# A linear-attention and SwiGLU block on one core: VectorE's side work by weight, earlier layer-norm of tiles 8 to 15, SyncE in written order, another place for wo

## The chip, the cores and the metric

One core of one Trainium2 chip. The metric is the device time of one execution in microseconds (us). TensorE is called PE, its weight loads PEld, VectorE DVE, ScalarE ACT, GpSimd POOL, SyncE SP; a `q` behind a name (SPq) is that engine's DMA issue. The kernel before takes 760.22 us, the median of three runs (759.44, 760.22 and 761.99).

## The reference

```python
xn = layernorm(x)                                  # x: 2048 tokens x 1024
q, k, v = split(xn @ wqkv)                         # 32 heads of 32
phi = lambda t: where(t > 0, t + 1, exp(t)) + 1e-6
kv  = einsum("bhsd,bhse->bhde", phi(k), v)         # sums over all tokens
z   = einsum("bhsd->bhd", phi(k))
o   = (phi(q) @ kv) / (phi(q) @ z + 1e-6)
s   = o @ wo
g   = silu((silu(xn @ w_gate) * (xn @ w_up)) @ w_down)   # hidden 3584
out = x + s * g
```

## The kernel before, in words

The 2048 tokens are 16 tiles of 128; four tiles are a block of 512 (block 2 is tiles 8 to 11, block 3 is tiles 12 to 15), two blocks are a pass of 1024. Three stages follow one another: the front (layer-norm, K, V, their sums, most of Q; about 0 to 163 us), the attention output (163 to 246 us), and the feed-forward part (from 246 us). The change lies in the front and at its seam with the attention output.

**Layer-norm.** `emit_stats` (line 331) takes a tile's statistics in two halves on DVE, `emit_aggr` (344) joins them, `emit_rstd` (358) gives 1/sqrt by three Newton steps on POOL or on DVE for a whole group of tiles (blocks 2 and 3 are one group each), and `emit_norm` (379) writes the normalised tile into `ws_all` as scratch. Tiles 0 to 7 are then turned by PE (`emit_T`, transposes at 405, copied out by DVE at 419 and ACT at 420). Blocks 2 and 3 are turned by DMA instead: `emit_xT_block` (422) stores the block to `xn_dram` (423) and loads it back transposed into `xnT` (424), both on SP.

**K and V, plain.** `emit_B(i, c)` (461) is eight matmuls of 512 columns (440) of tile i with column chunk c of the weights: c 0 and 1 are K, 2 and 3 are V. ACT makes exp and relu of K (186, 187), DVE joins them to phi (190, 191), ACT copies V (458). `emit_C(i)` (465) adds the tile to the sums `kvz` in PSUM. The loop over `rest` does so for tiles 4 to 7, 8 and 12.

**Q, K, V by seven products.** From tile 12's turn on, `QGroup` (211), and `KVGroup` (508) for tiles t of blocks 2 and 3 together, compute a 2x2 block product by seven products (Strassen-Winograd form) with sums of operands made beforehand on DVE: of the tokens (`xsum_ops`, 134, five operations of 128x2048), of wq (`wsum_ops`, 148, four smaller ones for each group), and of the K and V weights (`kv_sum_ops`, 487, five of 128x2048 each, two of them in place). `KVGroup(0, t)` is K of tiles 8+t and 12+t, `KVGroup(1, t)` is V of them; `VPlain` (709) is V of tiles 9 and 13 by plain matmuls. Each group has parts a, b, c and `post`; a group's part c is emitted behind part a of the next.

**What sets the order.** Under `tc.manual_schedule(engines=FRONT_ORDER)` (608) the instructions of PE, DVE, ACT and POOL stand in the order in which the code emits them; SP's order in the front is left to the scheduler, which puts both stores to `xn_dram` ahead of both transposes. DVE's side work (statistics, norms and sums of blocks 2 and 3) lies in a queue `later`; `fill(n)` (602) takes n operations from it, and the calls of `fill` between matmul groups, with the tables `fills` (678) and `seq` (727), spread them. In `seq` the groups come as Q1, K1, VPlain, Q2, K2, V2, Q3, K3, Q(1,0), V3, Q(1,1); a pair of tiles is added to `kvz` when its V is done.

**The seam.** The pools of the front close (`p1`) and those of the attention output open in their place (`p2`, 751): `otp`, `work`, `small`, then `wop` with wo. SP loads wo in two halves (846). `emit_ND` (774) divides and writes `o_sb` (795); `emit_OT` (804) stores it to `o_dram` (ACT, 808) and loads it back transposed (SP, 809); `emit_S` (814) multiplies by wo (822).

Of the kernel before, what the change touches and what calls it, by code (L numbers as in the profile page):

```python
# [12 lines left out]
BF16 = mybir.dt.bfloat16  # L13
# [8 lines left out]
def kernel(  # L22
# [11 lines left out]
    nc = tc.nc  # L34
    P = 128
    x2 = A_x.flatten_outer_dims()
    out2 = out.flatten_outer_dims()
    S, D = x2.shape
# [4 lines left out]
    DC = D // P  # L43
# [3 lines left out]
    NB = S // TB  # L47
# [61 lines left out]
    def xn_tok_ap(i):  # L109
        return xnT[i * P // SP_TOK][:, :, i * P % SP_TOK: i * P % SP_TOK + P]  # L110
# [153 lines left out]
    with ExitStack() as p1:  # L264
# [1 line left out]
        work = p1.enter_context(tc.tile_pool(name="p1work", bufs=4))  # L266
        small = p1.enter_context(tc.tile_pool(name="p1small", bufs=4))

        wkv_sb = wpool.tile([P, DC, 2 * D], BF16, name="wkv_sb")
        NV = 4  # L270
        v_bufs = [wpool.tile([P, G, NDW], BF16, name=f"v_sb{k}") for k in range(NV)]
        for k in range(NV):
# [11 lines left out]
        def load_x(i):  # L284
# [5 lines left out]
            eng = nc.scalar if i == 1 else nc.sync  # L290
            x_loads[i] = eng.dma_start(out=x_ap(i), in_=x2[i * P:(i + 1) * P, :])

        def load_wkv(c, halves=1):
            hs = DC // halves
            return [nc.sync.dma_start(out=wkv_sb[:, h * hs:(h + 1) * hs, c * CW:(c + 1) * CW],
                                      in_=wqkv_v[:, h * hs:(h + 1) * hs, D + c * CW: D + (c + 1) * CW])
                    for h in range(halves)]

# [27 lines left out]
        def emit_stats(i, parts=None):  # L326
            if i not in part_stats:
                part_stats[i] = small.tile([P, NSC, nc.vector.BN_STATS_DIM], FP32, name="stats", tag="stats")
            xr = x_ap(i).rearrange("p (c f) -> p c f", f=SCH)
            for c in (range(NSC) if parts is None else parts):  # L330
                nc.vector.bn_stats(out=part_stats[i][:, c, :], in_=xr[:, c, :])  # L331
            if parts is None:
                emit_aggr(i)

        def emit_aggr(i):
            gid = grp_of[i]
            tiles = GROUPS[gid]
            if gid not in grp_state:
                mv = small.tile([P, TPB, AGG], FP32, name="mv", tag="mv")
                rstd = small.tile([P, TPB], FP32, name="rstd", tag="rstd")  # L340
                grp_state[gid] = (mv, rstd, tiles)
            mv, rstd, _ = grp_state[gid]
            k = tiles.index(i)
            nc.vector.bn_aggr(out=mv[:, k, :], in_=part_stats.pop(i)[:])
            ln_state[i] = (mv, rstd, k)
# [44 lines left out]
        def xn_blk_slot(b):  # L390
            o = xn_base + b % 2 * TPB * D
            return ws_flat[:, o:o + TPB * D].rearrange("p (t d) -> p t d", t=TPB).bitcast(FP16)
# [44 lines left out]
        def emit_B_mm(i, c):  # L437
            kv_ps = psB.tile([P, CW], FP32, name="kv_ps", tag="B")
            for dc in range(DC):
                mm = nc.tensor.matmul(kv_ps[:], lhsT=xn_tok_ap(i)[:, dc, :], rhs=wkv_sb[:, dc, c * CW:(c + 1) * CW],  # L440
                                      start=(dc == 0), stop=(dc == DC - 1))
                if dc == 0 and c == 0:
                    marks[("B", i)] = mm
            kv_tiles[(i, c)] = kv_ps
# [40 lines left out]


        def kv_sum_ops(which, places):
            w = wkv_sb[:, :, which * D:(which + 1) * D]
            w11, w12, w21, w22 = w[:, 0:HD, 0:CW], w[:, 0:HD, CW:D], w[:, HD:DC, 0:CW], w[:, HD:DC, CW:D]
            s1, s5, s2 = places  # L490
            kv_rhs[which] = {"M4": lambda k: w22[:, k, :], "M3": lambda k: w11[:, k, :], "M1": lambda k: s1[:, k, :],
                             "M5": lambda k: s5[:, k, :], "M2": lambda k: s2[:, k, :],
                             "N7": lambda k: w21[:, k, :], "N6": lambda k: w12[:, k, :]}
            tt = nc.vector.tensor_tensor
            return [lambda: tt(out=s1, in0=w11, in1=w22, op=ALU.add), lambda: tt(out=s5, in0=w11, in1=w21, op=ALU.add),
                    lambda: tt(out=s2, in0=w12, in1=w22, op=ALU.add),
                    lambda: tt(out=w21, in0=w22, in1=w21, op=ALU.subtract),
                    lambda: tt(out=w12, in0=w11, in1=w12, op=ALU.subtract)]
# [9 lines left out]
        class KVGroup:  # L508
# [54 lines left out]
            def post(self):  # L563
                if self.which == 0:
                    for j in range(2):
                        emit_phi(self.pk[j][:], self.e[j][:])
                        pk_tiles[self.tiles[j]] = self.pk[j]
                else:
                    ready_C.extend(self.tiles)

        ready_C = deque()


        later = deque()

        def stats_ops(b):
            ops = []
            for i in range(b * TPB, (b + 1) * TPB):
                ops.append(lambda i=i: emit_stats(i, parts=(0,)))
                ops.append(lambda i=i: (emit_stats(i, parts=(1,)), emit_aggr(i)))  # L580
            return ops

        def norm_ops(b):
            return [lambda t=t: emit_norm(b * TPB + t, xn_blk_slot(b)[:, t, :]) for t in range(TPB)] + [lambda: emit_xT_block(b)]

        def ws_ops(m):
            return wsum_ops(wq_sb[:, :, m * FW:(m + 1) * FW], ws_all[:, m // 2, m % 2])

        later.extend(stats_ops(NB - 2) + [lambda: emit_rstd((NB - 2) * TPB)] + stats_ops(NB - 1))
        later.extend([lambda: emit_rstd((NB - 1) * TPB, nc.vector), None, None])  # L590
        for ops in (norm_ops(NB - 2), norm_ops(NB - 1), xsum_ops(0), ws_ops(0)):
            later.extend(ops)

        def more_ops():

            alloc_pqT()
            k_ops = kv_sum_ops(0, (pq_place(NPASS - 1, NM_Q - 2), pq_place(NPASS - 1, NM_Q - 1), x_quarter(0, 0, 1)))
            v_ops = kv_sum_ops(1, (x_quarter(0, 1, 0), x_quarter(1, 0, 1), x_quarter(1, 1, 0)))
            for ops in (ws_ops(1), xsum_ops(NPASS - 1), k_ops, v_ops[:1], ws_ops(2), v_ops[1:], ws_ops(3)):
                later.extend(ops)  # L600

        def fill(n):
            for _ in range(n):
                op = later.popleft() if later else None
                if op:
                    op()

        with tc.manual_schedule(engines=FRONT_ORDER):

            warm_up(14)  # L610
            emit_stats(0, parts=(0,))
# [26 lines left out]
            emit_B_mm(2, 0)  # L638
            emit_B_out(1, 2)
            emit_B_mm(2, 1)  # L640
            emit_T(3)
            emit_stats(TPB)
            emit_stats(TPB + 1)
            emit_rstd(TPB)
            emit_B_out(2, 0)
# [17 lines left out]
            emit_C(2)  # L663
            emit_B_out(3, 0)
            emit_B_mm(3, 1)
            emit_T(TPB)
            emit_B_out(3, 1)
            emit_N(TPB + 2)
# [6 lines left out]
            fill(2)  # L675

            rest = list(range(TPB, 2 * TPB)) + [b * TPB for b in range(2, NB)]
            fills = {2 * TPB: (2, 2, 1, 1), rest[-1]: (2, 2, 1, 1)}
            before = TPB - 1
            for i in rest:  # L680
                nf = fills.get(i, (3, 2, 2, 2))
                if i == 2 * TPB:
                    more_ops()
                grp = QGroup(0, 0) if i == rest[-1] else None
                emit_B(i, 0)
                fill(nf[0])
                emit_C(before)
                before = i
                if grp:
                    grp.part_a()  # L690
                emit_B(i, 1)
                fill(nf[1])
                if grp:
                    grp.part_b()
                if i == TPB:
                    emit_T(TPB + 2)
                emit_B(i, 2)
                fill(nf[2])
                if i == TPB:
                    emit_T(TPB + 3)  # L700
                if grp:
                    grp.part_c()
                emit_B(i, 3)
                if grp:
                    grp.post()
                fill(nf[3])

            K, V = (lambda t: KVGroup(0, t)), (lambda t: KVGroup(1, t))
            class VPlain:
# [7 lines left out]
                        emit_B(i, c)  # L717

                def part_c(self):
                    ready_C.extend(tiles1)  # L720

                def post(self):
                    pass

            tiles1 = [(NB - 2 + j) * TPB + 1 for j in range(2)]
            Q = QGroup
            seq = [(lambda: Q(0, 1), 1, 1), (lambda: K(1), 0, 1), (VPlain, 2, 2), (lambda: Q(0, 2), 1, 1),
                   (lambda: K(2), 1, 1), (lambda: V(2), 2, 2), (lambda: Q(0, 3), 0, 0), (lambda: K(3), 0, 0),
                   (lambda: Q(NPASS - 1, 0), 0, 0), (lambda: V(3), 0, 0), (lambda: Q(NPASS - 1, 1), 0, 0)]
            prev = None  # L730
            for make, fa, fb in seq:
# [17 lines left out]
        gate(wq_loads, marks[("B", 3)], sync=True)  # L749

    with ExitStack() as p2:
        otp = p2.enter_context(tc.tile_pool(name="p2oT", bufs=1))
        work = p2.enter_context(tc.tile_pool(name="p2work", bufs=2))
        small = p2.enter_context(tc.tile_pool(name="p2small", bufs=2))
        wop = p2.enter_context(tc.tile_pool(name="wop", bufs=1))
        oT_ab = otp.tile([P, 2, G, TB], BF16, name="oT")
        oT_cd = wq_sb[:].rearrange("p c n -> p (c n)").rearrange("p (b g t) -> p b g t", b=2, t=TB)
        s_tiles = {}
# [496 lines left out]
```

## Time and profile before

| | |
|---|---|
| median of three runs | 760.22 us |
| the profiled execution | 760.91 us |
| its span, first to last instruction | 759.1 us |
| PE busy | 743.6 us (98%) |
| DVE busy | 507.5 us (67%) |
| ACT busy | 275.9 us (36%) |
| POOL busy | 50.1 us (7%) |
| mean granted clock of PE | 0.996 |

The profiled execution is 0.69 us above the median, and 1.8 us of it lie outside the span. The share of busy time is taken over the whole program; single gaps of PE must be looked for in the view of waits (who waited for whom, in all, how often, longest) and then in the timeline (start, length, engine, line, operation, output<-input, count, and in brackets the idle time before it with what ended it). The view by stretches gives for each stretch the length, the busy time of PE, PEld, DVE, ACT and POOL with counts, then the granted clock, the DMA share and GB/s.

### The profile page before, as it was taken

What the parts mean: (1) busy time and instruction counts of PE and PEld (TensorE: products, weight loads), DVE (VectorE), ACT (ScalarE), POOL (GpSimd) and SP (SyncE); (2) the same over time, 40 slices, a digit from 0 to 9 for tenths busy, and PEclk for the clock granted to TensorE, in tenths of its full rate; (3) what the DMA queues carried; (4) which work ended last, traced back from release to release, by engine and by line L of the source; (5) the groups of instructions that cost most, each with busy time, mean ns of one, the idle gap of its engine ahead of it and who ended that gap; (6) DMA issues with size and microseconds to landing.
All of it is one profiled execution on the core that took longest, in us unless ns stands there. A gap on an engine that the chain in (4) does not pass through costs nothing.

```text
span 759.1 us, 9917 instructions
## 1 busy us (share of the span) xinstructions
PE 743.6 (98%) x3704; PEld 350.8 (46%) x3744; DVE 507.5 (67%) x939; ACT 275.9 (36%) x483; POOL 50.1 (7%) x101
## 2 busy tenths in 40 slices
PE   9998999998999999999999999999999999999997
PEld 4543444454554444444444444444444444444454
DVE  6697697686772578777687777776755754455453
ACT  4443475655423443343434334343433111111111
POOL 3310000000000000000000000000000221212220
PEclk9999999999999999999999999999999999999999
DMA  9608000035589635473354634553969854444300
GB/s 316 221 17 215 8 1 0 1 97 154 152 226 271 184 97 167 149 215 105 115 174 145 194 103 141 160 160 111 298 209 345 319 180 180 180 180 150 113 28 29
DMA packets 127664, 115.99 MB, mean 153 GB/s; under 512 B 29440, under 2 KB 108416, under 8 KB 126336
## 3 DMA queue, kind: packets, MB, share of 16 engines
q1 hardware_dynamic: 122720, 106.58, 44.8%
q10 hardware_dynamic: 4896, 8.78, 3.3%
q8 instruction: 29, 0.48, 0.2%
q14 instruction: 19, 0.16, 0.1%
HBM read 70.52 MB, written 38.54 MB: 144 GB/s over the span
## 4 chain that ended last, share of the span: by engine, by line
PE 91%; DVE 4%; DMA 3%; ACT 1%; issue 1%; DVEq 0%; ACTq 0%
PE X L131 29%; PE Y L131 28%; PE Z L131 10%; PE s_ps L822 7%; PE kv_ps L440 6%; PE qY L131 2%; PE qX L131 2%; PE kY L131 1%; PE kX L131 1%; DMA xnT<-xn_dram 1%; PE nd_ps L785 1%; PE kvz L469 1%; DVE stats L331 1%; DMA o_dram<-o_sb 1%; PE qZ L131 1%
## 5 line engine op out<-in xcount | busy, mean ns | idle before, releaser
L131 PEld LDWEIGHTS <-ws_all 128*128 128x128 bf16 x1420 | 137.6, 98 | 161.8 <-issue 0.2
L918 DVE TENSOR_TENSOR q<-n,Y 128x512 f32<-128x512 f32 x63 | 43.3, 688 | 107.7 <-PE Y L131 104.0
L131 PEld LDWEIGHTS <-xs 128*128 128x128 bf16 (+1 forms) x716 | 67.6, 98 | 75.3 <-issue 1.2
L440 PE MATMUL kv_ps<-wkv_sb,xnT 128*128 128x512 bf16 x342 | 79.8, 383 | 3.8 <-DMA xnT<-xn_dram 2.8
L1188 POOL TENSOR_TENSOR o_out<-y,xres 128x512 bf16<-128x512 f32 x29 | 35.1, 1212 | 669.1 <-DVE y L1187 669.1
L131 PE MATMUL Y<-xs,ws_all 128*128 128x512 f16 (+3 forms) x308 | 70.3, 360 | 0.0
L131 PE MATMUL X<-xnT,ws_all 128*128 128x512 f16 (+1 forms) x278 | 70.1, 379 | 0.2
L131 PE MATMUL Z<-xs,ws_all 128*128 128x512 f16 x224 | 57.5, 379 | 0.0
L131 PE MATMUL Y<-xnT,ws_all 128*128 128x512 f16 x224 | 57.5, 379 | 0.0
L131 PE MATMUL X<-xs,ws_all 128*128 128x512 f16 x224 | 57.5, 379 | 0.0
L1042 ACT ACTIVATE g<-cg 128x512 bf16<-128x512 f32 x56 | 35.3, 630 | 53.7 <-DVE cg L933 53.7
L924 DVE TENSOR_TENSOR u<-Z,q 128x512 f32<-128x512 f32 x63 | 43.3, 687 | 16.0 <-PE Z L131 15.9
L440 PEld LDWEIGHTS <-xnT 128*128 128x128 f16 x352 | 33.9, 99 | 42.7 <-DMA xnT<-xn_dram 3.3
L1042 ACT ACTIVATE g<-X 128x512 bf16<-128x512 f32 x28 | 16.7, 597 | 99.7 <-PE X L131 99.7
L914 ACT COPY n<-X 128x512 f32<-128x512 f32 x63 | 36.9, 585 | 28.7 <-PE X L131 28.7
L1067 DVE TENSOR_TENSOR ho<-g,up 128x1024 bf16<-128x1024 bf16 x56 | 38.2, 686 | 0.5
L1187 DVE TENSOR_TENSOR y<-y,s_in 128x512 f32<-128x512 f32 x31 | 22.2, 717 | 20.7 <-ACT y L1181 15.8
L131 PEld LDWEIGHTS <-wg_sb 128*128 128x128 bf16 x224 | 21.9, 98 | 26.4
L131 PEld LDWEIGHTS <-wu_sb 128*128 128x128 bf16 x224 | 21.9, 98 | 26.4
L826 ACT CAST s_sb<-s_ps 128x512 bf16<-128x512 f32 x32 | 18.5, 585 | 40.8 <-PE s_ps L822 36.1
L822 PE MATMUL s_ps<-wo_sb,oT 128*128 128x512 bf16 x123 | 29.0, 379 | 3.2 <-DMA oT<-o_dram 3.0
L1181 ACT ACTIVATE y<-X 128x512 f32<-128x512 f32 x8 | 4.8, 597 | 69.7 <-PE X L131 61.2
(173 smaller groups left out, 1101.9 us busy)
## 6 DMA issues: line engine op xcount, KB each, us to landing
h_dram<-ho SPq DMA_DIRECT2D x56, 256.0 KB, 2.5
wg_sb<-in_B_w_gate_dram SPq DMA_DIRECT2D x14, 512.0 KB, 3.9
wu_sb<-in_B_w_up_dram SPq DMA_DIRECT2D x14, 512.0 KB, 4.2
wdr<-in_B_w_down_dram SPq DMA_DIRECT2D x14, 512.0 KB, 4.0
ws_all<-h_dram SPq DMA_DIRECT2D x4, 1792.0 KB, 9.0
wds_dram<-wdsA SPq DMA_DIRECT2D x14, 384.0 KB, 2.6
hp_a<-h_dram SPq DMA_DIRECT2D x3, 1792.0 KB, 7.3
o_dram<-o_sb ACTq DMA_DIRECT2D x16, 256.0 KB, 2.9
```

The lines of the kernel that those rows point to most:

```text
L131: marks["mm"] = nc.tensor.matmul(acc[:, 0:c1 - c0], lhsT=lhs(k), rhs=rhs(k)[:, c0:c1], start=(first and k == 0), stop=(k == n - 1), skip_g ...
L331: nc.vector.bn_stats(out=part_stats[i][:, c, :], in_=xr[:, c, :])
L440: mm = nc.tensor.matmul(kv_ps[:], lhsT=xn_tok_ap(i)[:, dc, :], rhs=wkv_sb[:, dc, c * CW:(c + 1) * CW], start=(dc == 0), stop=(dc == DC - 1))
L822: mm = nc.tensor.matmul(s_ps[:], lhsT=oT[:, c, ttok], rhs=wo_sb[:, c, cc * CW:(cc + 1) * CW], start=(c == 0), stop=(c == G - 1))
L826: nc.scalar.copy(out=s_sb[:, cc * CW:(cc + 1) * CW], in_=s_ps[:])
L914: nc.scalar.copy(out=n[:], in_=self.X[:])
L918: nc.vector.tensor_tensor(out=self.q[:], in0=n[:], in1=self.Y[:], op=ALU.add)
L924: nc.vector.tensor_tensor(out=self.u[:], in0=Z[:], in1=self.q[:], op=ALU.add)
L1042: nc.scalar.activation(out=self.g[:, i, j * TB:(j + 1) * TB], in_=src, func=ACT.Silu)
L1067: nc.vector.tensor_tensor(out=self.ho[:, i], in0=self.g[:, i], in1=self.up[:, i], op=ALU.mult)
L1187: nc.vector.tensor_tensor(out=t[:], in0=t[:], in1=self.s_in[:, i, cs], op=ALU.mult)
L1188: (nc.vector if last and (i, j) != (0, 0) else nc.gpsimd).tensor_tensor(out=self.o_out[:, i, cs], in0=t[:], in1=self.xres[:, i, cs], op=AL ...
```

## The change

- `later` now holds pairs of a weight and an operation. `fill(n)` adds n to a credit and takes operations, each paid with its weight, while the credit is above zero. Statistics and norms weigh 1, DVE's Newton steps 4, wq's sums 0.75, the 128x2048 sums 2, the DMA turn of a block 0.
- Queue order: statistics of block 2, its 1/sqrt (POOL), statistics of block 3, norms of block 2 with its turn, 1/sqrt of block 3 (DVE), norms of block 3 with its turn, then all sums.
- `emit_stats(TPB)` (tile 4) moves ahead of the copy of tile 3's transpose, and a new `fill(4)` stands ahead of the copy of tile 4's transpose.
- `seq` becomes Q1, VPlain, K1, Q2, V2, K2, Q3, K3, Q(1,0), V3, Q(1,1), with other fills; a pair of tiles is now added to `kvz` when both its K and its V are done (`have`).
- SP, too, stands in written order in the front: store of block 2, its transpose, store of block 3, its transpose.
- `wkv_sb` is split into `wk_sb` and `wv_sb`, and `wop` is the first pool of `p2`, so that `wo_sb` gets the bytes of `wk_sb`.

The instructions of PE, ACT and POOL are the same in number and kind; on DVE they are too. Their order changes.

```diff
-        wkv_sb = wpool.tile([P, DC, 2 * D], BF16, name="wkv_sb")
+        wkv_sb = [wpool.tile([P, DC, D], BF16, name=n) for n in ("wk_sb", "wv_sb")]
...
-                else:
-                    ready_C.extend(self.tiles)
+                have(self.tiles)
 
         ready_C = deque()
+        half = set()
+
+        def have(tiles):
+
+            if tiles[0] in half:
+                ready_C.extend(tiles)
+            half.add(tiles[0])
...
-        later.extend(stats_ops(NB - 2) + [lambda: emit_rstd((NB - 2) * TPB)] + stats_ops(NB - 1))
-        later.extend([lambda: emit_rstd((NB - 1) * TPB, nc.vector), None, None])
-        for ops in (norm_ops(NB - 2), norm_ops(NB - 1), xsum_ops(0), ws_ops(0)):
-            later.extend(ops)
...
-            for ops in (ws_ops(1), xsum_ops(NPASS - 1), k_ops, v_ops[:1], ws_ops(2), v_ops[1:], ws_ops(3)):
-                later.extend(ops)
-
-        def fill(n):
-            for _ in range(n):
-                op = later.popleft() if later else None
-                if op:
-                    op()
-
-        with tc.manual_schedule(engines=FRONT_ORDER):
+        def put(weight, ops):
+            later.extend((weight, op) for op in ops)
+
+        def fill(n):
+            credit[0] += n
+            while later and credit[0] > 0:
+                weight, op = later.popleft()
+                credit[0] -= weight
+                op()
...
+            put(2, xsum_ops(0))
+            put_ws(0)
+            put_ws(1)
+            put(2, xsum_ops(NPASS - 1))
+            put(2, k_ops)
+            put_ws(2)
+            put(2, v_ops[:1])
+            put_ws(3)
+            put(2, v_ops[1:])
+
+        put_stats(NB - 2)
+        put(1, [lambda: emit_rstd((NB - 2) * TPB)])
+        put_stats(NB - 1)
+        put_norms(NB - 2)
+        put(4, [lambda: emit_rstd((NB - 1) * TPB, nc.vector)])
+        put_norms(NB - 1)
+        put(0, [put_sums])
+
+        with tc.manual_schedule(engines=FRONT_ORDER | {ET.SP}):
...
             emit_B_mm(2, 1)
+            emit_stats(TPB)
             emit_T(3)
-            emit_stats(TPB)
...
             emit_B_mm(3, 1)
+            fill(4)
             emit_T(TPB)
...
-            fills = {2 * TPB: (2, 2, 1, 1), rest[-1]: (2, 2, 1, 1)}
+            fills = {rest[-1]: (2, 3, 2, 2)}
...
-                if i == 2 * TPB:
-                    more_ops()
...
                 def part_c(self):
-                    ready_C.extend(tiles1)
+                    have(tiles1)
...
-            seq = [(lambda: Q(0, 1), 1, 1), (lambda: K(1), 0, 1), (VPlain, 2, 2), (lambda: Q(0, 2), 1, 1),
-                   (lambda: K(2), 1, 1), (lambda: V(2), 2, 2), (lambda: Q(0, 3), 0, 0), (lambda: K(3), 0, 0),
+            seq = [(lambda: Q(0, 1), 1, 1), (VPlain, 4, 6), (lambda: K(1), 1, 1), (lambda: Q(0, 2), 1, 1),
+                   (lambda: V(2), 3, 3), (lambda: K(2), 1, 1), (lambda: Q(0, 3), 1, 0), (lambda: K(3), 0, 0),
...
     with ExitStack() as p2:
+        wop = p2.enter_context(tc.tile_pool(name="wop", bufs=1))
         otp = p2.enter_context(tc.tile_pool(name="p2oT", bufs=1))
         work = p2.enter_context(tc.tile_pool(name="p2work", bufs=2))
         small = p2.enter_context(tc.tile_pool(name="p2small", bufs=2))
-        wop = p2.enter_context(tc.tile_pool(name="wop", bufs=1))
```

More of the change, by code (lines that the diff above doesn't have):

```diff
@@ L291, in load_x, with wkv_ap @@
             x_loads[i] = eng.dma_start(out=x_ap(i), in_=x2[i * P:(i + 1) * P, :])
+        def wkv_ap(c):
+            return wkv_sb[c // NCC][:, :, c % NCC * CW:(c % NCC + 1) * CW]
         def load_wkv(c, halves=1):
             hs = DC // halves
-            return [nc.sync.dma_start(out=wkv_sb[:, h * hs:(h + 1) * hs, c * CW:(c + 1) * CW],
+            return [nc.sync.dma_start(out=wkv_ap(c)[:, h * hs:(h + 1) * hs, :],
                                       in_=wqkv_v[:, h * hs:(h + 1) * hs, D + c * CW: D + (c + 1) * CW])
@@ L439, in emit_B_mm @@
             for dc in range(DC):
-                mm = nc.tensor.matmul(kv_ps[:], lhsT=xn_tok_ap(i)[:, dc, :], rhs=wkv_sb[:, dc, c * CW:(c + 1) * CW],
+                mm = nc.tensor.matmul(kv_ps[:], lhsT=xn_tok_ap(i)[:, dc, :], rhs=wkv_ap(c)[:, dc, :],
                                       start=(dc == 0), stop=(dc == DC - 1))
@@ L487, in kv_sum_ops @@
         def kv_sum_ops(which, places):
-            w = wkv_sb[:, :, which * D:(which + 1) * D]
+            w = wkv_sb[which]
             w11, w12, w21, w22 = w[:, 0:HD, 0:CW], w[:, 0:HD, CW:D], w[:, HD:DC, 0:CW], w[:, HD:DC, CW:D]
@@ L567, in post, with put_stats, put_norms, put_ws @@
                         pk_tiles[self.tiles[j]] = self.pk[j]
-                else:
-                    ready_C.extend(self.tiles)
+                have(self.tiles)
         ready_C = deque()
-        later = deque()
-        def stats_ops(b):
-            ops = []
-            for i in range(b * TPB, (b + 1) * TPB):
[L579 to L587, printed above, removed]
-        later.extend(stats_ops(NB - 2) + [lambda: emit_rstd((NB - 2) * TPB)] + stats_ops(NB - 1))
-        later.extend([lambda: emit_rstd((NB - 1) * TPB, nc.vector), None, None])
-        for ops in (norm_ops(NB - 2), norm_ops(NB - 1), xsum_ops(0), ws_ops(0)):
-            later.extend(ops)
-        def more_ops():
+        half = set()
[3 more added lines that the diff above has]
+            half.add(tiles[0])
+        later = deque()
+        credit = [0]
+        def put(weight, ops):
[6 more added lines that the diff above has]
+                op()
+        def put_stats(b):
+            for i in range(b * TPB, (b + 1) * TPB):
+                put(1, [lambda i=i: emit_stats(i, parts=(0,)), lambda i=i: (emit_stats(i, parts=(1,)), emit_aggr(i))])
+        def put_norms(b):
+            put(1, [lambda t=t: emit_norm(b * TPB + t, xn_blk_slot(b)[:, t, :]) for t in range(TPB)])
+            put(0, [lambda: emit_xT_block(b)])
+        def put_ws(m):
+            put(0.75, wsum_ops(wq_sb[:, :, m * FW:(m + 1) * FW], ws_all[:, m // 2, m % 2]))
+        def put_sums():
             alloc_pqT()
```

## The prediction, made before the changed kernel ran

> **What bounds the kernel now.** The page comes first: PE is busy for 98% of the span, and the change neither adds nor removes an instruction on any engine. It can gain only where PE stands still or runs at a lower clock, so the next view is that of PE's waits.
>
> ```profile
> PE 743.6 (98%) x3704; PEld 350.8 (46%) x3744; DVE 507.5 (67%) x939; ACT 275.9 (36%) x483; POOL 50.1 (7%) x101
> ...
> PE s_ps L822 <- DMA oT<-o_dram: 3.0, 1, 3.0
> PE kv_ps L440 <- DMA xnT<-xn_dram: 2.8, 1, 2.8
> ```
>
> Two waits matter, each happens once, and both are for a DMA transpose. The stretches around the second line (length, busy PE, PEld, DVE, ACT, POOL, granted clock, DMA share, GB/s) show its price:
>
> ```profile
> 65.00:70.67 5.67, 5.67 (x33) 2.58 (x30) 5.57 (x8) 2.76 (x5) 0.00 (x0) 1.00 1.10 271
> 70.67:73.50 2.83, 0.01 (x2) 0.01 (x1) 2.25 (x6) 0.58 (x1) 0.00 (x0) 1.00 1.07 208
> 73.50:77.42 3.92, 3.70 (x16) 2.02 (x18) 0.00 (x0) 0.68 (x2) 0.00 (x0) 0.56 0.95 215
> ```
>
> PE is idle for 2.83 us before tile 8, and then works at a mean clock of 0.56: in quarter-microsecond stretches the clock is 0.50 from 74.0 to 77.4. Half a clock for 3.42 us loses 1.7 us. **Gap 1 costs 4.5 us.** The timeline says why the transpose is late:
>
> ```profile
> 58.14 1.91 DVE L379 TENSOR_SCALAR ws_all<-xp,mv,rstd 128x1024 f16<-128x1024 bf16 x4
> 60.07 3.91 SPq L423 DMA_DIRECT2D xn_dram<-ws_all  x2
> 61.66 1.91 DVE L379 TENSOR_SCALAR ws_all<-xp,mv,rstd 128x1024 f16<-128x1024 bf16 x4
> 64.45 10.66 SPq L424 DMA_TRANSPOSE xnT<-xn_dram  x2
> ```
>
> The norms of block 2 end at 60.05, its store lands 4.4 us later, and its transpose, beside the store of block 3 (issued 63.59), takes 9.0 us more. The chain, for both gaps:
>
> ```profile
> 60.07 4.36 DMA xn_dram<-ws_all
> 64.45 9.01 DMA xnT<-xn_dram
> ...
> 168.37 6.17 DMA o_dram<-o_sb
> 174.56 3.54 DMA oT<-o_dram
> ```
>
> Gap 2 (175.16 to 178.14, 2.98 us, clock 1.00 throughout) waits for the first `o_sb`, whose store takes 6.2 us, against 2.9 in the median of its kind, because wo's 2 MB (issued from 163.62) use the DMA engines.
>
> **Part 1: statistics and norms sooner.** I walked DVE's new order with old durations. It puts work into two idle stretches:
>
> ```profile
> 21.20:23.57 2.37, 2.32 (x17) 1.32 (x17) 0.00 (x1) 0.00 (x0) 0.00 (x0) 1.00 1.03 379
> 32.90:35.75 2.85, 2.85 (x26) 1.78 (x25) 0.01 (x1) 1.08 (x2) 1.99 (x11) 1.00 1.02 343
> ```
>
> A tile's statistics take 1.39 us (starts at 39.72, 41.16, 42.55). Tile 4's fit the first stretch. Tiles 8 and 9 (2.8 us) fit the second; since tile 4's moved up, they may begin 1.2 us earlier, so the copies of both transposes stay on time. The x loads are issued by 21.0 and their traffic is over by about 26. If that cover were short, PE would notice only beyond several microseconds, as tile 4's matmuls begin at 41.68. From 39.72 DVE goes: tiles 10, 11 to 42.6; three 1/sqrt operations of 0.2 to 43.2; tile 12 to 44.6; phi 1.2 to 45.8; tile 13 to 47.1; a copy; tile 14 to 48.85; a copy; tile 15 to 50.6. POOL's twelve Newton operations (0.28 apart) run from 43.2 to 46.6, beside this. Three norms of 0.48 end at 52.0, a phi that waits for ACT (53.15, as now) ends at 54.4, the fourth norm at 54.9, against 60.05. So the store lands at 54.9 + 4.4 = 59.3 and the transpose 6.5 to 9.0 us later (the two rows of L424), at 65.8 to 68.3. PE needs it at 70.67. Gap 1 goes with its clock drop: **-2.8 and -1.7**.
>
> **Part 2: SP in written order.** What is late next is block 3. DVE has its 1/sqrt at 57.8 (15 operations, 2.9 us) and its norms at 59.7 (1.91), but its store now stands behind block 2's transpose in SP's queue. That instruction starts at 59.3 and holds SP 4.5 to 6.1 us (the two rows). Store from 63.8 to 65.4; landing 4.4 to 5.3 later (two rows), 68.2 to 70.7; transpose landed 6.5 to 9.0 later: 74.7 to 79.7. PE, no longer stopped, wants block 3 after four chunks of 1.73 and one C of 0.46: at 70.67 + 7.4 = 78.05. I take the shorter ends (75.3), since the 9.0 was beside another megabyte: no wait. The far end is a wait of 1.65 us. Of DVE's sums behind it only the first needs block 2 alone and precedes phi of tile 8, so that phi is not held.
>
> **Part 3: sums by weight, VPlain first.** The five sums of 128x2048 at 1.16 each stay what they are; the walk finds DVE 0.2 us late for the second product of Q1 (now it is ready 0.07 us ahead): **+0.2**. Beside VPlain and Q1's part c (10.4 us of PE) DVE has about as much work; K1's first addition is done at 108.5 with PE asking at 109.2, so a further delay of 0.7 costs nothing. New is that K comes last for tiles 9/13 and 10/14, so `kvz` waits for phi instead of copies of V. The chain is Q3's:
>
> ```profile
> 143.10 1.03 PE L131 MATMUL qY<-xs,ws_all 128*128 128x512 f16 x4
> 143.30 0.69 DVE L251 TENSOR_TENSOR pqT<-qu,qX 128x512 bf16<-128x512 f32 x1
> ...
> 146.53 0.69 DVE L191 TENSOR_TENSOR pqT<-e_t,pqT 128x1024 bf16<-128x1024 bf16 x1 [0.15 <-ACT pqT L187]
> ```
>
> Part c's last matmul ends at 143.97 (kZ's start), the second phi at 147.22: 3.25 us. PE has part b (3 x 0.864) and one C (0.46) to fill it, 3.05; with the hand-over a wait of 0.3, twice: **+0.6**. Queued behind it are the next group's matmuls, so it counts in full. The old 0.4 (kX, waiting for ACT's v_sb) I leave standing: it arises from ACT's queue, which is as long as before.
>
> **Part 4: wo in the place of K's weights.** If the load began once K3's matmuls are over (150.0) it would be done before `o_sb` is stored, and gap 2 (-3.0) would go. I cost it at **nothing**: in both built programs the first wo load waits for the same instructions, the last kvz matmul, the last two writes of `v_sb` by DVE and ACT, and POOL's memset of `v_sb`, although its address is now exactly K's weights. The wait seems to be that of the whole pool, not of the tile. In the profile:
>
> ```profile
> SPq L846 <- PE kvz L469: 88.4, 1, 88.4
> ```
>
> **Sum.** -2.8 - 1.7 + 0.2 + 0.6 = -3.7 on the profiled execution's 760.9 gives **757.2**. That execution lies 0.7 above the median, and runs spread from 759.4 to 762.0; a clock drop in one run and not in another would explain as much, so I do not correct for it. Against the median 760.22 it is -0.4%.
>
> **Rivals.** (a) *The clock drop moves to gap 2*, now some 4 us earlier: 757.2 + 1.7 = 758.9. For it: the same idle length drew it at gap 1. Against: gap 2 did not draw it. [...]
>
> (b) *Slower: block 3 falls strictly behind block 2.* If store 3 moved only after transpose 2 has landed, the far ends add up: 59.3 + 9.0 + 5.3 + 9.0 = 82.6, PE waits 4.5 us at tile 12 and the clock drops, 6.2 in all: 763.4. It hurts from 78.05 on and has eaten the gain when block 3 lands at about 80. Against: store 3 landed in 5.3 beside transpose 2, and transpose 3's own traffic lasted only some 4 us (72.8 to 76.5). [...]
>
> (c) *DVE late beside VPlain:* one 1.16-us sum too many ahead of K1 and again ahead of V2, less 0.7 of slack each time, is 0.9 in all: 758.1. For: DVE is busy nearly all of that stretch; against: the walk.
>
> (d) *wo does load early:* 754.2. Only the waits of the built program speak against it, strongly.
>
> (e) *The change does not do what it says:* part 4 is that already; for part 1 it would need late x loads, which the DMA row excludes.
>
> **How the numbers follow.** Forecast 0.53, (a) 0.24, (b) 0.12, (c) 0.05, (d) 0.06. The range leaves out (b) and (d): low 757.2 less the 0.7 above the median and a run's 0.8 below it, about 755.5; high (a) or the far end of part 2 (758.9) plus 1.8, about 760.7. A change of 0.3% (2.3 us, below 757.9) is about what a measurement of this kernel tells from none. Forecast mostly, (d) and a little of (a) are faster: 0.60; most of (a) and (c), the rest of the forecast and a little of (b): 0.28; the rest of (b): 0.12.
>
> **What would show it.** Store 2 near 55, transposes near 59 and 70; no line "kv_ps <- DMA xnT" among PE's waits and clock 1.00 from 60 to 100; kvz waiting for pk_sb (L191's DVE) about 0.3 us twice; wo still released by the last kvz matmul and gap 2 still near 3 us. I am wrong if wo starts before the sums end, if tile 12 waits, or if DVE shows up as PE's releaser for more than about a microsecond.

## The result, and the profile after

The changed kernel takes **755.37 us**, the median of six runs (754.11 to 756.88), against 760.38 (758.89 to 762.31) for the kernel before in six runs: a ratio of 0.9933 with a 95% interval of 0.9912 to 0.9954. It is faster by 5.0 us, and the median lies 0.1 us below the low end of the predicted range. The profiled execution took 754.58 us with a span of 752.8. One later execution of the kernel after, of eight in the run e8_after_again, took 1125.69 us at a mean clock of 0.656, and no ratio below counts it.

The busy times, from the page of the kernel after:

```profile
PE 744.0 (99%) x3744; PEld 350.2 (47%) x3744; DVE 508.3 (68%) x939; ACT 276.1 (37%) x483; POOL 51.1 (7%) x101
```

and PE's waits (who waited for whom, in all, how often, longest):

```profile
PE s_ps L844 <- DMA oT<-o_dram: 1.6, 1, 1.6
PE w_ps L482 <- DVE warm L90: 1.2, 1, 1.2
PE kv_ps L444 <- DVE xnT L423: 0.5, 1, 0.5
PE kvz L473 <- ACT v_sb L462: 0.5, 1, 0.5
```

PE's busy time is what it was; the line of the wait for `xnT<-xn_dram` is gone, and the wait for `oT` is half as long. The stretches around the old gap 1 (same columns as in the prediction):

```profile
66.00:70.67 4.67, 4.67 (x23) 2.13 (x22) 4.09 (x9) 1.89 (x4) 0.00 (x0) 1.00 0.56 176
70.67:73.50 2.83, 2.83 (x21) 1.54 (x19) 2.80 (x6) 1.58 (x3) 0.00 (x0) 1.00 1.27 287
73.50:77.42 3.92, 3.92 (x20) 1.75 (x18) 2.03 (x3) 1.76 (x4) 0.00 (x0) 1.00 0.01 2
```

PE is busy all through at a clock of 1.00. The timeline of DVE's norms and of SP's queue (kernel after; start, length) shows why:

```profile
50.57 1.41 DVE L383 TENSOR_SCALAR ws_all<-xp,mv,rstd 128x1024 f16<-128x1024 bf16 x3
54.30 0.54 DVE L383 TENSOR_SCALAR ws_all<-xp,mv,rstd 128x1024 f16<-128x1024 bf16 x1
54.87 0.39 SPq L427 DMA_DIRECT2D xn_dram<-ws_all  x1
57.74 1.92 DVE L383 TENSOR_SCALAR ws_all<-xp,mv,rstd 128x1024 f16<-128x1024 bf16 x4
59.43 4.01 SPq L428 DMA_TRANSPOSE xnT<-xn_dram  x1
63.54 0.52 SPq L427 DMA_DIRECT2D xn_dram<-ws_all  x1
68.18 4.02 SPq L428 DMA_TRANSPOSE xnT<-xn_dram  x1
```

Block 2's store is issued at 54.87, its transpose at 59.43 and landed 6.1 us later; block 3's go at 63.54 and 68.18. The chain around gap 2 (kernel after):

```profile
163.45 4.98 DMA o_dram<-o_sb
168.44 3.30 DMA oT<-o_dram
171.79 1.90 PE s_ps L844 x8
```

Four points of PE's work tell where the time went. They are the start of the first matmul of Q(0,0), of the first `nd_ps`, of the first `s_ps` and of the feed-forward part:

| execution | Q(0,0) | nd_ps | s_ps | feed-forward | end |
|---|---|---|---|---|---|
| before | 84.73 | 165.68 | 178.14 | 246.32 | 759.1 |
| after | 80.07 | 160.76 | 171.79 | 239.97 | 752.8 |

Up to Q(0,0) the change gains 4.66 us, from there to `nd_ps` 0.26 (80.69 against 80.95), at gap 2 1.43 (11.03 against 12.46), and nothing behind it (68.18 both times, then 512.8 both times). The first figure scatters by execution: in the other profiles of the kernel after and its variants, none of which has gap 1, Q(0,0) starts between 79.8 and 80.6. The second does not. The questions are why the middle stretch became shorter, where I had forecast +0.8, and whether the shorter gap 2 belongs to the change.

### The profile page after: what moved, and what is told of

Same layout as the page of the kernel before. It is cut to its first block, busy times and chain, and to the rows that moved or that the text cites. A ratio compares the mean times of both kernels' runs of the same rounds, so it can differ in the third digit from the quotient of the medians.

```text
span 752.8 us, 9958 instructions
## 1 busy us (share of the span) xinstructions
PE 744.0 (99%) x3744; PEld 350.2 (47%) x3744; DVE 508.3 (68%) x939; ACT 276.1 (37%) x483; POOL 51.1 (7%) x101
## 4 chain that ended last, share of the span: by engine, by line
PE 94%; DVE 3%; DMA 1%; ACT 1%; issue 0%; DVEq 0%; ACTq 0%
PE X L131 29%; PE Y L131 29%; PE Z L131 10%; PE kv_ps L444 9%; PE s_ps L844 7%; PE qY L131 2%; PE qX L131 2%; PE kX L131 2%; PE kY L131 1%; PE nd_ps L807 1%; PE kvz L473 1%; DVE stats L335 1%; PE w_ps L482 1%; DMA o_dram<-o_sb 1%; PE kZ L131 1%; PE qZ L131 1%
## 5 line engine op out<-in xcount | busy, mean ns | idle before, releaser
L444 PE MATMUL kv_ps<-wv_sb,xnT 128*128 128x512 bf16 x192 | 44.0, 379 | 0.0
L444 PE MATMUL kv_ps<-wk_sb,xnT 128*128 128x512 bf16 x160 | 37.3, 379 | 0.5 <-DVE xnT L423 0.5
```

## The experiments

Each run is compared with the kernel before run in the same session, whose median there lay between 759.7 and 761.5. All diffs are against the kernel after unless another is named. "Tile by tile" means that wo's pool waits for the users of the bytes its tile takes, not for all of the pools that it replaces:

```diff
-        wop = p2.enter_context(tc.tile_pool(name="wop", bufs=1))
+        wop = p2.enter_context(tc.tile_pool(name="wop", bufs=1, reuse_waits="tile"))
```

### First set: parts of the change taken back

**e1_old_seq**, the old order of the groups:

```diff
-            seq = [(lambda: Q(0, 1), 1, 1), (VPlain, 4, 6), (lambda: K(1), 1, 1), (lambda: Q(0, 2), 1, 1),
-                   (lambda: V(2), 3, 3), (lambda: K(2), 1, 1), (lambda: Q(0, 3), 1, 0), (lambda: K(3), 0, 0),
+            seq = [(lambda: Q(0, 1), 1, 1), (lambda: K(1), 1, 1), (VPlain, 4, 6), (lambda: Q(0, 2), 1, 1),
+                   (lambda: K(2), 1, 1), (lambda: V(2), 3, 3), (lambda: Q(0, 3), 1, 0), (lambda: K(3), 0, 0),
```

> The changed kernel with K1 ahead of VPlain and K2 ahead of V2 again (the fills stay with the groups they name). The stretch from tile 12's Q group to K3 gained 0.26 us net in the profiles, with two new waits of 0.28 us (kvz for phi of tiles 13 and 14) in it. Theory A, the order of V matters little: the two waits go, the old small waits (0.8 us in all) come back, the time is 755.6, same within 0.3%. Theory B, VectorE needs V of (9,13) first to have K's weight sums ready: K1's third product waits for the sum in place of K's weights, PE stalls more than 1 us before K1's parts b and c, and the time is 757 or more.

Measured: 755.74 us (753.85 to 757.91), ratio 0.9945 [0.9925, 0.9965]. The middle stretch takes 80.41, 0.28 less than with the new order. The sums `kvz` of the tiles 9/13 and 10/14, in the kernel after:

```profile
115.06 1.36 PE L473 MATMUL kvz<-v_sb,pk_sb 128*128 128x129 bf16 x16
134.39 1.36 PE L473 MATMUL kvz<-v_sb,pk_sb 128*128 128x129 bf16 x16
```

and with the old order:

```profile
115.08 1.09 PE L473 MATMUL kvz<-v_sb,pk_sb 128*128 128x129 bf16 x16
134.13 1.08 PE L473 MATMUL kvz<-v_sb,pk_sb 128*128 128x129 bf16 x16
```

The two waits for phi that part 3 of the prediction priced at 0.3 each are there, 0.28 each, and go with the old order (x16 takes 1.36 with the wait in it and 1.09 without). The old order has one stall of 0.27 of its own in Q2, so that the new order costs 0.28 in all. This is no scatter: the stretch takes 80.41 in all three executions with the old order (e1, e5, e7), 80.67 to 80.69 in all seven with the new one, and 80.94 to 80.97 in all four of the kernel before and its variants. The old wait of kX for `v_sb` (0.37, with 0.16 around it) does not come back with the old order; so it was not the order of the groups that removed it. The kernel before shows what made it (DVE, then ACT and PE):

```profile
130.02 0.69 DVE L540 TENSOR_TENSOR qu<-qu,kY 128x512 f32<-128x512 f32 x1
130.63 0.42 DVE L152 TENSOR_TENSOR ws_all<-wq_sb 128x512 bf16<-128x512 bf16 x1
130.96 0.68 DVE L153 TENSOR_TENSOR ws_all<-wq_sb 128x1024 bf16<-128x1024 bf16 x1
131.56 0.68 DVE L557 TENSOR_TENSOR pk_sb<-qu,kX 128x512 bf16<-128x512 f32 x1
...
132.28 0.63 ACT L186 ACTIVATE e_t<-pk_sb 128x512 bf16<-128x512 bf16 x1 [2.29 <-DVE pk_sb L557]
...
134.66 0.57 ACT L531 CAST v_sb<-kX 128x512 bf16<-128x512 f32 x1
135.28 1.02 PE L131 MATMUL kX<-wkv_sb,xs 128*128 128x512 bf16 x4 [0.37 <-ACT v_sb L531]
```

and the same place in e1_old_seq:

```profile
124.44 0.69 DVE L544 TENSOR_TENSOR qu<-qu,kY 128x512 f32<-128x512 f32 x1
125.05 0.68 DVE L561 TENSOR_TENSOR pk_sb<-qu,kX 128x512 bf16<-128x512 f32 x1
...
125.76 0.63 ACT L186 ACTIVATE e_t<-pk_sb 128x512 bf16<-128x512 bf16 x1 [1.35 <-DVE pk_sb L561]
...
128.14 0.57 ACT L535 CAST v_sb<-kX 128x512 bf16<-128x512 f32 x1
```

In the kernel before two of wq's sums stand on DVE between `qu` and K2's `pk_sb`; ACT waits 2.29 us for `pk_sb` and its cast of `v_sb`, queued behind the phi of K2, comes too late for PE. In e1 all of wq's sums are done by 111.3 us, ACT waits 0.94 less, and PE does not wait. What moved them is the new queue of DVE's side work. Its order, its weights and the numbers in `fill` changed together, and no run tells them apart.

**e2_wo_last**, wo's pool opened last as before (its place is then that of the V copies):

```diff
-        wop = p2.enter_context(tc.tile_pool(name="wop", bufs=1))
         otp = p2.enter_context(tc.tile_pool(name="p2oT", bufs=1))
         work = p2.enter_context(tc.tile_pool(name="p2work", bufs=2))
         small = p2.enter_context(tc.tile_pool(name="p2small", bufs=2))
+        wop = p2.enter_context(tc.tile_pool(name="wop", bufs=1))
```

> The changed kernel with wo's pool opened last again, as before the change. My theory: the place of wo does nothing, since its first load waits for the last kvz matmul in either place; the 1.4 us by which gap 2 was shorter in the changed kernel's profile (1.55 against 2.99 us) are chance of that execution. Then the time is that of the changed kernel within 0.3% (755.4, ratio to before 0.993), wo's load is released by the last kvz matmul, and gap 2 lies anywhere between 1.5 and 3 us. Rival: the new place of wo (or of oT and o_sb behind it) makes the transfers faster; then gap 2 is back at 3.0 us, the first o_dram store near 6.2 us, and the time is 1.4 us longer, about 756.8.

Measured: 755.51 us (754.05 to 758.42), ratio 0.9944 [0.9925, 0.9962]: the place of wo is worth nothing that the time shows. But the profile has gap 2 at 3.1 us, as the kernel before, and this one difference was followed up in the third set.

**e3_wo_tile**, the kernel after with wo's wait taken tile by tile (the diff above).

> The changed kernel with wo's pool set to wait for single tiles instead of whole pools, so that wo's load waits only for the last matmul that reads K's weights. My theory: gap 2 is the first o_dram store beside wo's 2 MB. The load then starts near 145 us and is over before 155; the store at 163.4 takes about 2.9 us instead of 5 to 6, the transpose 3.3, oT is there at 169.7, ahead of PE's 170.2: gap 2 goes (0 to 0.3 us), and with it the chance of a clock drop there. Time 752.5, between 751.5 and 753.8. Rival: the store is slow by itself (cold path, o_sb's place); then the store still takes 5 us or more, gap 2 stays at 1.5 to 3 us and the time at 755.4.

Measured: **752.86 us** (752.55 to 753.53), ratio 0.9908 [0.9893, 0.9923]; faster than both kernels, and in a narrow band. From the waits of SP's queue in this run:

```profile
SPq L868 <- PE kY L131: 48.2, 1, 48.2
```

wo is released by K3's last matmul and issued at 145.1 instead of 158.7; behind the first `o_sb` store, now alone, its transpose is issued after 3.2 us (163.27, 166.48; 4.99 in the kernel after) and PE has no wait at gap 2: `s_ps` follows `nd_ps` after 9.32 us, against 11.03. So the wait that part 4 of the prediction read off the built programs is that of the pool, and it is this wait, not the bytes, that keeps wo's load late.

**e5_norms_only**: the earlier statistics and norms and the fills by weight alone; the groups in the old order, SP's front left to the scheduler, wo's pool last (the diffs of e1 and e2, and the line below).

```diff
-        with tc.manual_schedule(engines=FRONT_ORDER | {ET.SP}):
+        with tc.manual_schedule(engines=FRONT_ORDER):
```

> The changed kernel without three of its parts: K1 ahead of VPlain and K2 ahead of V2 again, SP left to the scheduler in the front, wo's pool last. What is left is VectorE's queue by weight with the earlier statistics and norms. My theory: this part alone takes gap 1 away (2.8 us and 1.7 us of half clock), so nearly the whole gain is here: 755.9, between 754.8 and 757.0, with no wait of PE for xnT. Rival: the order of SP or of the groups is needed for the gain; then PE waits for xnT again (1 us or more) or at kvz and the K groups, and the time is 757.5 or more.

Measured: 757.15 us (753.97 to 757.69), ratio 0.9955 [0.9937, 0.9973], just above the range that I had expected. PE has no wait for `xnT`, so the earlier norms alone remove gap 1. But in this execution the clock drop came at gap 2 (columns as above):

```profile
170.50:173.31 2.81, 0.00 (x2) 0.01 (x1) 1.30 (x3) 2.00 (x4) 0.00 (x0) 1.00 0.67 152
173.31:177.50 4.19, 4.19 (x18) 2.16 (x19) 0.70 (x4) 0.99 (x2) 0.00 (x0) 0.59 0.51 136
```

That is the prediction's rival (a), and it costs 1.5 us: from `s_ps` to the feed-forward part it takes 69.70 instead of 68.18.

### Second set: wo's load early, to take gap 2 out of the comparison

**e6_before_wo**, the kernel before with the split of `wkv_sb`, wo's pool first and its wait tile by tile; nothing else.

> The kernel before with nothing changed but wo's load: K's and V's weights in two tiles, wo's pool opened first so that wo lies in K's weights, and its wait taken tile by tile, so that it waits for K3's last matmul alone and is issued some 18 us sooner. Gap 1 stays as it was (PE waits about 2.8 us for xnT, then half clock). Theory A, the two gaps are separate and add: gap 2's 2.99 us go, nothing else moves, 760.2 less 3.0 = 757.2, and the spread of the runs shrinks, because a run can no longer draw a clock drop at gap 2 (range 756.3 to 757.8). Theory B, what gap 2 costs is set by the work after it (the first FFN weights or the attention's DVE chain wait anyway): the time gained before the first s_ps is given back, S0 to FFN grows, and the run is within 0.3% of before, 758.5 to 760.5.

Measured: 757.57 us (755.6 to 758.2), ratio 0.9952 [0.9935, 0.9968]. Theory A holds: from `nd_ps` to `s_ps` it takes 9.31 and from there 68.15, while gap 1 stands, with half clock behind it (a mean of 0.59 from 73.82 to 77.60):

```profile
PE kv_ps L444 <- DMA xnT<-xn_dram: 2.9, 1, 2.9
```

The two gaps are separate.

**e7_old_seq_tile**, the diffs of e1 and e3 together.

> The changed kernel with the old order of the groups (K1 ahead of V of tiles 9 and 13, K2 ahead of V2) and wo's wait taken tile by tile. Theory A, the new order of the groups costs 0.28 (kvz waits for phi) and the fills by weight removed the old small stalls: the stretch from Q00 to the first nd_ps is 80.41, against 80.68 with the new order, and the time is 752.86 - 0.28 = 752.6 (752.1 to 753.0), the fastest version so far. Theory B, the difference of the two orders was chance: 80.7 and 752.9. Theory C, the tile wait moves wo's 2 MB load beside what the old order reads from DMA there: the stretch grows by over 0.5, 753.5 or more.

Measured: 752.74 us (752.34 to 752.96), ratio 0.9889 [0.9862, 0.9917]; the middle stretch is 80.41 again. Theory A, though 0.1 us of time does not tell it from e3.

**e10_sp_sched_tile**, the kernel after without SP's written order (the diff of e5) and with wo's wait tile by tile.

> The changed kernel with SyncE's front left to the scheduler again (both xn_dram stores, then both transposes) and wo's wait taken tile by tile, so that gap 2 cannot blur it. Theory A, with the statistics and norms sooner the written order is not needed: the second store holds SyncE until about 60.5, block 2's transpose is issued there and lands by 69, before PE wants it at about 70.7; time 752.9 (752.4 to 753.5), the same as with the written order. Theory B, the written order is a needed part: the two transposes in flight together bring block 2's past 70.7, PE waits 0.5 to 2 us, and with a wait of over 1 us a half-clock stretch can follow (+1.7): 753.5 to 756.5.

Measured: 753.11 us (752.55 to 753.45), ratio 0.9894 [0.9869, 0.9919], the same as e3. SP's queue in this run:

```profile
54.60 5.20 SPq L427 DMA_DIRECT2D xn_dram<-ws_all  x2
59.90 11.09 SPq L428 DMA_TRANSPOSE xnT<-xn_dram  x2
```

With both stores first, block 2's transpose takes 9.1 us again and lands at 69.0, still ahead of PE. Once the norms are early, the written order is worth nothing that the time shows. The half clock that theory B attaches to a wait of over 1 us followed none of the seven gaps of 1.05 to 1.76 us in the profiles.

**e8_after_again**, the kernel after once more.

> The changed kernel once more, for a second profile of gap 2 and more times. Theory A, wo's place decides how long the first o_dram store and its transposition take: with wo first, gap 2 is again 1.3 to 1.7 us and the store about 4.9. Theory B, the length is drawn anew in each execution: any value from 1.3 to 3.1, the store from 4.9 to 6.2. Times 755.4 (754.0 to 757.0), in two bunches (about 754.5 and 756.7) by whether a clock drop follows gap 2.

Measured: ratio 0.9932 [0.9905, 0.996]. The store takes 4.61 us and gap 2 is 1.25. Seven times fall in two bunches: 754.05 to 754.99 at a mean clock of 1.00, and 756.9 to 759.1 at 0.995 to 0.997.

### Third set: does wo's place shorten gap 2?

**e12_before_wo_pool**: e6 with wo's wait left to the pool. **e11_oT_wo**: the kernel after with `otp` opened ahead of `wop`. **e9_wo_last_again**: e2 once more.

> The kernel before with wo's place alone changed: K's and V's weights in two tiles and wo's pool opened first, its wait left to the whole pool, so that it is still released by the last kvz matmul. Theory A, the place by itself shortens gap 2: the first o_dram store lands in about 5.0 instead of 6.17, PE waits 1.3 to 1.7 instead of 2.99, and S0 - ND0 is about 11.0 instead of 12.46; the time is about 1.4 under before, some 758.8, gap 1 unchanged. Theory B, the place does nothing and the shorter store belongs to another part of the change (the order of SyncE, or the time that the kernel gained ahead): store 5.9 to 6.2, gap 2 2.8 to 3.1, time 760.2.

> The changed kernel with oT's pool first and wo's second, so that oT takes K's weights' place and wo lies 16 KB per partition higher, o_sb where it is in the changed kernel. Theory A1, what counts is where wo lies relative to what was there (it must lie in K's weights): gap 2 is near 3.0, the store near 6, time about 756.5. Theory A2, what counts is where o_sb lies, or that wo is not the last pool: gap 2 stays 1.3 to 1.7, time 755.4. Theory B, chance: either.

> The changed kernel with wo's pool opened last, once more, for a second profile. Theory A, the place decides: gap 2 again 2.8 to 3.1, store about 5.9, S0 - ND0 12.4 to 12.6. Theory B, drawn anew in each execution: anything from 1.3 to 3.1. Time 755.5 to 756.5 either way.

Measured: e12 759.76 us, ratio 0.9993 [0.998, 1.0005]; e11 754.55, ratio 0.9941 [0.9921, 0.996]; e9 754.35, ratio 0.9934 [0.9914, 0.9954]. The decisive pair is e2 and e9, one program in two executions. The chain in e2, whose gap 2 is 3.1 us:

```profile
163.22 5.90 DMA o_dram<-o_sb
169.14 3.94 DMA oT<-o_dram
```

and in e9, where it is 1.1:

```profile
163.15 4.76 DMA o_dram<-o_sb
167.93 3.04 DMA oT<-o_dram
```

My theory that the place decides falls: gap 2 is 3.1 and 1.1 us in the same program, and with wo in K's place it is 1.55 and 1.25 (after) and 1.4 (e1), but 2.6 in e12. With oT there it is 1.8 (e11). Its length is drawn in each execution. What draws it is open: wo's issue leads the store by 4.74 or 4.75 us in every one of them.

The profile of e12 is worth a look for the clock. Gap 1 and what follows it, then gap 2 and what follows it:

```profile
71.19:73.63 2.44, 0.00 (x1) 0.00 (x1) 2.25 (x6) 0.58 (x1) 0.00 (x0) 1.00 1.04 228
73.63:77.50 3.87, 3.81 (x23) 2.04 (x25) 0.00 (x0) 1.09 (x2) 0.00 (x0) 1.00 1.11 225
173.62:176.24 2.62, 0.01 (x2) 0.01 (x1) 1.31 (x3) 1.81 (x4) 0.00 (x0) 1.00 0.74 161
176.24:180.50 4.26, 4.21 (x18) 2.23 (x20) 1.16 (x5) 1.18 (x2) 0.00 (x0) 0.64 0.46 125
```

Here the drop skips gap 1 and comes at gap 2. From the end of gap 1 to Q(0,0) it takes 9.57 us, against 11.23 in the kernel before, and the attention output takes 1.53 longer: nearly the same price at another place.

### Last run: SP's order alone

**e13_before_sp**, the kernel before with SP in written order in the front:

```diff
-        with tc.manual_schedule(engines=FRONT_ORDER):
+        with tc.manual_schedule(engines=FRONT_ORDER | {ET.SP}):
```

> The kernel before with one thing changed: SyncE's front in written order, so that block 2's transpose goes ahead of block 3's store; statistics, norms, groups and wo stay as before. Theory A, block 2's transpose was long because block 3's store ran beside it (9.0 us in three profiles with both stores first, 6.1 alone): issued at 64.45 it now lands at about 70.5, PE's wait for xnT at 70.67 is gone or under 0.5 us; block 3's store starts when the transpose has left SyncE, at about 68.5, lands at 73.1 and is transposed by 79.2, so that PE waits some 1.2 us at tile 12 (78.05) instead, with or without a half-clock stretch after it: 757.1, or 758.8 with the stretch (756.5 to 759.3). Theory B, the store decides when block 2 is there, and the transpose takes as long as before: gap 1 stays 2.4 to 2.9 us and block 3 adds a wait of its own: 760.0 to 763.4.

Measured: 757.04 us (755.55 to 758.36), ratio 0.9967 [0.9949, 0.9986]. Theory A, nearly to the tenth. SP's queue in this run, and the first matmuls of tile 12, which have to wait:

```profile
59.81 0.39 SPq L423 DMA_DIRECT2D xn_dram<-ws_all  x1
64.19 4.09 SPq L424 DMA_TRANSPOSE xnT<-xn_dram  x1
68.38 0.52 SPq L423 DMA_DIRECT2D xn_dram<-ws_all  x1
73.03 3.90 SPq L424 DMA_TRANSPOSE xnT<-xn_dram  x1
79.02 1.90 PE L440 MATMUL kv_ps<-wkv_sb,xnT 128*128 128x512 bf16 x8 [1.05 <-DMA xnT<-xn_dram]
```

Without the other store ahead of it in the queue block 2's transpose needs 6.2 us instead of 9.0, and PE's wait for it is gone with nothing else changed; block 3, now behind, makes PE wait 1.05 us at tile 12. Both transfers are SP's, and no run puts that store on another queue, so the order within the queue and the sharing of the DMA engines are not told apart as the cause of the 9.0 against 6.2.

## Why the prediction was right in its direction and short by 1.8 us

- **Part 1, gap 1: right.** -4.5 forecast, -4.66 measured (4.1 to 5.0 by the other executions). The walk along DVE's new order gave the store at 54.9 and the norms of block 3 at 59.7; the trace has 54.87 and 59.66. e5 shows that this part alone takes the gap away.
- **Part 2: right, and its value was misjudged as none.** Block 3 lands before PE asks for it, as forecast with the shorter ends, because each transpose now starts with no store still under way ahead of it in SP's queue (6.0 and 6.1 us, not 6.5 to 9.0). The shortest ends as stated add up to 74.7, not 75.3; it landed at 74.2. I priced SP's order only as a risk. By itself it is worth 0.33% (e13), beside the earlier norms nothing (e10): both remove the same gap, and their gains do not add. Rival (b) did not come: block 3's store landed 4.6 us after its issue, although block 2's transpose was under way for the first 2.0 of them.
- **Part 3: the step that failed.** Forecast +0.8, measured -0.26. The two waits of `kvz` came as priced (0.28 each); the +0.2 at the second product of Q1 did not. What failed is the sentence "The old 0.4 (kX, waiting for ACT's v_sb) I leave standing: it arises from ACT's queue, which is as long as before." ACT's queue was as long, but it was late because it waited for DVE, and DVE's new queue changed just that. With two smaller stalls of 0.17 and 0.10 in K2, some 0.8 us that I had left standing were gone. The mis-sizing of this term is 1.06 us.
- **Part 4: right.** wo waits for the last `kvz` matmul as before (the row of SP's queue below again names `kvz`), and its place is worth nothing: e2 and e9 by time, e12 by ratio 0.9993. The 1.43 us by which gap 2 is shorter in the profile of after is what one execution drew, not the change. My statement that gap 2 would stay "near 3 us" was wrong for another reason: the 3.0 of the one profile of before was near the long end of a range from 1.1 to 3.1. SP's wait for wo in the kernel after:

```profile
SPq L868 <- PE kvz L473: 86.4, 1, 86.4
```

- **Sum: the base.** "I do not correct for it" cost 0.53: the profiled execution of before (760.91) lies that much above the six-run median. Median 760.38, less 4.66 and 0.26, is 755.46; measured 755.37. That they meet to 0.1 is partly luck, since both medians hold runs with and without a clock drop.
- **Rival (a)** is real: the drop came at gap 2 in e5 and e12. But it is drawn anew in each execution: the fourteen executions of the kernel before in e13's session have mean clocks from 0.994 to 1.000, and the two bunches of e8 fit it. Its argument from "the same idle length" does not hold: no half clock followed gaps of 2.99 and 3.11 us, and one followed a gap of 2.62 us (the last section). The drop therefore belongs to both kernels, and is a reason for the spread rather than a price of the change. With neither gap (e3, e7, e10) the times lie within 1.0 us or less; with gap 2 they spread over 2.8 (after), 4.1 (e1) and 4.4 us (e2), though the four times of e9 lie within 1.0 too.
- **Rivals (c) and (d)** did not come: the stretch became shorter, and wo was not early. Where wo is early (e3), the time is 2.5 us below that of the kernel after, and (d) had put 3.0 on it.
- **The range** ended at the forecast less the base and one run's scatter; 757.2 less 0.7 and 0.8 is 755.7, so the low end of 755.5 is not quite its own sum. A gain in the middle stretch had no case in it, although three stalls stood in the trace there.

## What to carry to other kernels

A wait that the change "leaves standing" has to be followed one releaser further: an engine's queue that is as long as before can still run earlier, because what it waits for has moved. Two edits that remove the same gap must not be added, and one of them may be spare; each should be priced alone. Where a pool takes over the memory of several others, look at what its first DMA waits for, not only at the bytes it lands in: here the wait, one argument in the code, was worth more than the place.

## What the runs showed of the hardware

- In the four executions with a drop at a gap (before, e6, e5, e12) the granted clock is halved for 3.4 us (3.41 in before; a loss of 1.5 to 1.7 us), and it falls 0.5, 0.7, 0.8 and 1.2 us after the gap has ended. The length of a gap does not decide whether the drop comes. The gaps of over 2 us, and the mean granted clock of the stretch of 3.8 to 4.3 us behind each:

| gap | length | granted clock behind it | half clock |
|---|---|---|---|
| gap 2, e2 | 3.11 | 1.00 | no |
| gap 2, before | 2.99 | 1.00 | no |
| gap 1, e6 | 2.91 | 0.59 | yes |
| gap 1, before | 2.83 | 0.56 | yes |
| gap 2, e5 | 2.81 | 0.59 | yes |
| gap 2, e12 | 2.62 | 0.64 | yes |
| gap 1, e12 | 2.44 | 1.00 | no |

So the two longest gaps got off free and a gap of 2.62 us did not, and the seven gaps of 1.05 to 1.76 us had no half clock behind them. What decides it is not shown; no run was made to test it.
- A store of 256 KB beside wo's 2 MB load takes between 4.56 and 6.17 us in ten executions. In the four without it (e3, e6, e7, e10) the transpose behind that store is issued 3.1 to 3.2 us after it.
- A transpose of 1 MB takes 6.0 to 6.2 us in the kernel after and in e13, where no store ahead of it in its queue is still under way, and 8.6 to 9.3 when one is (block 2's, in the five executions with both stores first).
